# An mLSTM cell and a multiplicative FFN on one core: the denominators' product on GpSimd, and three more units of y by way of DRAM

## The chip, the core and the metric

The kernel runs on one core of one Trainium2 chip, all in float32. The core has five engines, each with a queue of its own that it works through in order: TensorE (PE; loading weights, PEld, overlaps its matmuls), VectorE (DVE), ScalarE (ACT), GpSimd (POOL) and SyncE (SP), which here only issues DMAs. They meet at semaphores. The metric is the device time in microseconds, the median of several executions. Durations and starts below come from one profiled execution; starts are counted from the start of its span.

## The reference

For each of 4 batches and 8 heads an mLSTM cell runs over 768 steps; its output, laid out as 3072 tokens x 320, goes through a feed-forward net that multiplies two linear maps.

```python
for t in range(S):
    m_new = np.maximum(f_gate[:, :, t] + m, i_gate[:, :, t])
    f_stab = np.exp(f_gate[:, :, t] + m - m_new)
    i_stab = np.exp(i_gate[:, :, t] - m_new)
    C = f_stab * C + i_stab * outer(v_t, k_t)
    n = f_stab * n + i_stab * k_t
    h_tilde, nq = C @ q_t, n . q_t
    denom = np.maximum(np.abs(nq), 1.0)
    y[:, :, t] = sigmoid(o_gate[:, :, t]) * h_tilde / denom
x = y.transpose(0, 2, 1, 3).reshape(3072, 320)
out = ((x @ w1) * (x @ w2)) @ w3 @ w_out          # d_ff = 1024
```

(The loop is shortened: indices of batch and head are left out.)

## The kernel before

**Units and passes.** The steps are cut into chunks of 64, and two chunks of one batch make a *unit*: 128 tokens, all 8 heads. There are 24 units; unit n is batch n % 4, pair of chunks n // 4. One loop, `for s in range(len(n_up))`, makes 32 *passes*. Pass s loads ahead for units s + 2 and s + 3, does the scores and the state update of unit s, the outputs of unit s - 1, brings the output of an earlier unit into the layout that the FFN needs, and puts FFN work in between. Four units, one for each batch, make a *group* of 512 tokens; the FFN works group by group.

**The cell in a pass (`quarter_work`).** PE multiplies into two PSUM tiles `cell`: for unit n = s - 1 the weighted values (`ph`) and what the states before give (`pi`); for unit s the scores (`ss`) and the two states' increments (`pc`). All matmuls are recorded on L92, all transposes by PE on L95. DVE then goes through this list, in this order:

- L423, L430 (four): `h` = `pi` times a gate column, plus `ph`. `h` has 41 columns a head; the 41st is the denominator's sum.
- L438: absolute value of that column, into `den`.
- L397: scores of unit s times their weights (`first_read`: what follows is issued after it).
- L440: maximum with 1, times 2.
- L404 (L406 for the first four units): first increment into `state`; POOL then multiplies this state by its decay (L335, `decayed`), into the next state.
- L441: reciprocal of `den`.
- L414: second increment into that next state. It waits for L335.
- L443: `e = (tanh + 1) * den`, in place in `o_in`, with `den` broadcast over a head's 40 columns.
- L445: `y = h * e`.

`outputs` is a generator that hands out the `den` steps one at a time, so that `quarter_work` can put other work between them; `late` is a hook that in pass 3 converts a piece of the weights (`convert`: L199, L200) at two places of the list, the second time the remainder `wr`. The last four units have one increment only, so no L335 and L414 in the middle.

**From y to x.** The FFN needs y with the features on the partitions. There are two ways. Units below `NY` = 15: POOL copies the last 64 columns a second time (`twice`, L476), PE transposes three blocks of 128 columns (`x_trans`, L95, tile `px`), ACT copies the result to `xT` (L486). Units from `NY` on: SP writes y to DRAM in four DMAs (`send`, L456 and L458), reads it back in four, with 32x32 blocks in place (`get_back`, L465, one buffer `yb`), and DVE turns the blocks (`x_turn`, L472). In pass s that is for unit s - 2, `send` at the pass's head, `get_back` after the pass's loads, `x_turn` after the outputs. Units 12 to 15 are the fourth group, of which three now go through PE.

**SP's queue.** In a pass SP issues `send`, the rows of U for `pw` of unit s + 3 (L159), k, v and o for unit s + 2 (L139, L153), `get_back`, then k and q of unit s + 2 in turned blocks (`load_turned`, L148), which DVE transposes in the next pass (`turn`, L317). Each waits for its data or buffer and holds up what is behind it.

**POOL's queue.** In a pass: L335 for the decay of the state, a second L335 in the middle of the cell's work, `vw` (L330, values times weights, for the next unit), masks on `pw` (L308, two), and `twice`. In passes 16 and 17 come four sums of weights each (L659).

**The FFN.** Groups 0 to 2 are computed straight (`up`, L638, L639). Groups 3 to 5 go by seven products instead of eight (`up_by_seven`): DVE makes four differences of tokens a group (`token_sums`, L666, into `w3T`), in passes 17, 21 and 25; PE makes the products; ACT copies two of them to `wo` (L702, L704, called `kept`), DVE adds (L686, L684), POOL finishes `kept` (L711, two), DVE adds the rest (L686, L684, into `a_sb` and `ab`), and POOL multiplies the two halves (L729, two). The same is done for the output (`out_by_seven`), with sums of the output weights on POOL (L755, one in pass 24, three in pass 25) and of `ab` on DVE (`ab_sums`, L770). The code puts L729 and L755 behind the outputs of the pass:

```python
        with tc.issue_after(gated.ins) if gated else nullcontext():
            if seven:
                seven[3]()
            for _ in range({NU: 1, NU + 1: 3}.get(s, 0)):
                next(wsums)
```

**What sets the order.** PE's order is the order of the code (`in_order`). Elsewhere each engine takes its instructions in the order in which they stand in its queue, which follows the code and the `issue_after` hints.

Of the kernel before, what the change touches and what calls it, by code (L numbers as in the profile page):

```python
# [11 lines left out]
OP = mybir.AluOpType  # L12
# [4 lines left out]
def kernel(  # L17
# [26 lines left out]
    nc = tc.nc  # L44

    B, H, S, D = q.shape
    L = 64
    P = 128
# [6 lines left out]
    DM = H * D  # L55
# [21 lines left out]
    def mps(shape, name):  # L77
        pool = banks.pop(0)
        banks.append(pool)
        return pool.tile(shape, FP, name=name, tag="m")  # L80
# [10 lines left out]
    def mm(out, lhsT, rhs, start=True, stop=True):  # L91
        in_order(nc.tensor.matmul(out, lhsT=lhsT, rhs=rhs, start=start, stop=stop))  # L92
# [4 lines left out]
    def warm(n, m=4, small=0):  # L97
        bank = mps([P, 4, P], "fill")
        for _ in range(n):
            mm(bank[:, 0:m], ident, ident.unsqueeze(1).to_broadcast([P, m, P]))  # L100
        for i in range(small):
            r = halves[i % 2]
            mm(bank[r, 0, 0:L], ident[r, 0:L], ident[r, 0:L])
# [8 lines left out]
    N_DIAG = 2  # L112
# [10 lines left out]
    decay = const.tile([P, B * NP, NT], FP, name="decay")  # L123
    UT = const.tile([P, 2, 3, BH], FP, name="UT")
    U_d = dram.tile([NT, BH, L], FP, name="U_d")
    NY = 15
    KC = KF + 1
    y_d = [dram.tile([P, 4, KC, 32], FP, name=f"y_d{n}") if n >= NY else None for n in range(NU)]

# [137 lines left out]
    qT_t, kT_t, vw_t, before_t, y_t, x_t = {}, {}, {}, {}, {}, {}  # L267
# [65 lines left out]
    def decayed(new, old, n, x):  # L333
        c, b = divmod(n, B)
        nc.gpsimd.tensor_tensor(out=new, in0=old, op=OP.mult, in1=decay[:, b * NP:(b + 1) * NP, 2 * c + x:2 * c + x + 1]  # L335
                                .to_broadcast([P, NP, D1]))

    def quarter_work(s, rest, between, late):


        rest()

        def part(j, c0, n):
            return cell[j][:, :, c0:c0 + NP * n].rearrange("p x (n d) -> p x n d", d=n)

        ss, pc, pi = part(0, 0, L), part(0, NP * L, D1), part(1, 0, D1)
        ph = [cell[1][:, x, NP * D1:2 * NP * D1].rearrange("p (h d) -> p h d", d=D1) for x in range(2)]
        n = s - 1
        if 0 <= n < NU:
            pw, vt, qT = u_t.pop(n), vbuf[n % NBV], qT_t.pop(n)  # L350
            before = before_t.pop(n)
            if n < N_DIAG:
                warm(1)

            if n < N_DIAG:
                ph = mps([P, H, D1], "ph")
                for hq in range(H):
                    for r in halves:
                        mm(ph[r, hq, :], pw[r, hq, :], vt[r, hq, :])
            for hd in range(H // 2 if n >= N_DIAG else 0):  # L360
                for x, e in quarters:
                    hq = hd if x == e else hd + H // 2
                    mm(ph[x][halves[e], hd, :], pw[halves[x], hq, :], vt[halves[x], hq, :])
            for p in range(NP):
                for hip, x in quarters if n >= B else quarters[1:3]:
                    mm(pi[halves[x], hip, p, :], qT[heads[hip], p, halves[x]], before[x][heads[hip], p, :])
        den = None
        if 0 <= s - 1 < NU:
            den = outputs(s - 1, pi, ph)
            den()  # L370
            if between:
                for _ in range(3):
                    den()
                den = None
                between()
            if late:
                late()
        n, first_read = s, None
        if n < NU:
            c, b = divmod(n, B)  # L380
            kt, vw = kbuf[n % NB], vw_t.pop(n)
            ends = range(2 if c < NT2 - 1 else 1)
            first, second, after = state[b]
            before_t[n] = first, second
            state[b] = after, second, first
            kT, qT, pw = kT_t.pop(n), qT_t[n], u_t[n]
            for p in range(NP):
                for hip, x in quarters:
                    mm(ss[halves[x], hip, p, :], kT[heads[hip], p, halves[x]], qT[heads[hip], p, halves[x]])
            M = D if n else L  # L390
            for p in range(NP):
                for x, e in quarters:
                    if x in ends:
                        mm(pc[e * L:e * L + M, x, p, :], kt[halves[x], 2 * p + e, 0:M], vw[halves[x], 2 * p + e, :])
        if n < NU:
            pv = pw.rearrange("p (n two) t -> p two n t", two=2)
            first_read = nc.vector.tensor_tensor(out=pv, in0=ss, in1=pv, op=OP.mult)  # L397
        with tc.issue_after(first_read.ins) if first_read else nullcontext():
            if den:
                den()  # L400
            if n < NU:

                if c:
                    nc.vector.tensor_tensor(out=second, in0=pc[:, 0], in1=second, op=OP.add)  # L404
                else:
                    nc.vector.tensor_copy(out=second, in_=pc[:, 0])  # L406
                if len(ends) > 1:
                    decayed(after, second, n, 1)
            if late:
                late()  # L410
            if den:
                den()
            if n < NU and len(ends) > 1:
                nc.vector.tensor_tensor(out=after, in0=pc[:, 1], in1=after, op=OP.add)  # L414
            if den:
                done = den()
        return done if den else first_read

    def outputs(n, pi, ph):
        c, b = divmod(n, B)  # L420
        hs = slice(b * H, (b + 1) * H)
        h = sb.tile([P, H, D1], FP, name="h", tag="h")
        nc.vector.tensor_tensor(out=h.rearrange("p (n two) d -> p two n d", two=2), in0=pi,  # L423
                                in1=gT[:, c, hs].rearrange("p (n two) -> p two n", two=2).unsqueeze(3)
                                .to_broadcast([P, 2, NP, D1]), op=OP.mult)
        if n < N_DIAG:
            nc.vector.tensor_tensor(out=h, in0=ph, in1=h, op=OP.add)
        for x, e in quarters if n >= N_DIAG else ():
            part = h[halves[x], 0:H // 2] if x == e else h[halves[x], H // 2:H]
            nc.vector.tensor_tensor(out=part, in0=ph[x][halves[e]], in1=part, op=OP.add)  # L430

        den = sb.tile([P, H, 1], FP, name="den", tag="den")

        def steps():
            V = nc.vector
            yield V.tensor_scalar(out=den.bitcast(U32), in0=h[:, :, D:D1].bitcast(U32), scalar1=0x7FFFFFFF, scalar2=None,  # L438
                            op0=OP.bitwise_and)
            yield V.tensor_scalar(out=den, in0=den, scalar1=1.0, scalar2=2.0, op0=OP.max, op1=OP.mult)  # L440
            yield V.reciprocal(out=den, in_=den)  # L441
            e = o_t.pop(n)
            nc.vector.scalar_tensor_tensor(out=e, in0=e, scalar=1.0, in1=den.to_broadcast([P, H, D]), op0=OP.add, op1=OP.mult)  # L443
            y_t[n] = sb.tile([P, DM + REM], FP, name="y", tag="y")
            yield nc.vector.tensor_tensor(out=y_t[n][:, 0:DM].rearrange("p (h d) -> p h d", d=D), in0=h[:, :, 0:D],  # L445
                                           in1=e, op=OP.mult)

        done = steps()
        return lambda: next(done)

# [24 lines left out]
    def twice(n):  # L475
        nc.gpsimd.tensor_copy(out=y_t[n][:, DM:DM + REM], in_=y_t[n][:, KF * P:DM])  # L476
# [83 lines left out]
    V = nc.vector  # L560
# [7 lines left out]
    for i, r in enumerate(third):  # L568
        V.tensor_tensor_scan(out=M[r, 1:GC + 1], data0=F3[r, :, L - 1], data1=U3[r, :, L - 1], initial=M[r, 0:1],
                             op0=OP.add, op1=OP.max)  # L570
# [24 lines left out]
    for i, r in enumerate(third):  # L595
        nc.gpsimd.tensor_tensor(out=pick[r, :, i, :], in0=pair[r].to_broadcast([BH, B * NP, GC]), op=OP.mult,
                        in1=dec[r].unsqueeze(1).to_broadcast([BH, B * NP, GC]))
# [222 lines left out]
    for s in range(len(n_up)):  # L820
        if NY <= s - 2 < NU:
            send(s - 2)
# [19 lines left out]
        if s < NU:  # L842
            if s >= B:
                decayed(state[s % B][1], state[s % B][0], s, 0)
        if s == 2 or N_DVE < s < NY + 2:
            twice(s - 2)
        if NY <= s - 2 < NU:
            get_back(s - 2)
        while s >= N_DVE and turned < min(s - 2, NY):
            x_trans(turned)  # L850
# [32 lines left out]
        def rest():  # L883
            for x in open_ups:
                up_rest(*x)
            if seven:
                seven[2]()
            if s == 3:
                scale_next()
                scale_next()  # L890
# [27 lines left out]
        with tc.issue_after(gated.ins) if gated else nullcontext():  # L918
# [4 lines left out]
            if s == NU + 1:  # L923
                ab_sums(*summed.pop(0))
            if NY <= s - 2 < NU:
                x_turn(s - 2)
# [85 lines left out]
```

## Time and profile before

| | |
|---|---|
| time, median of 3 runs | 426.37 us (426.09 to 426.73) |
| profiled execution, span | 425.8 us |
| mean granted clock of TensorE | 0.996 |
| DMA moved | 51.15 MB, mean 120 GB/s |
| L443, DVE, 24 times | 17.4 us, 725 ns each (491 to 1295) |
| L445, DVE, 24 times | 17.0 us, 709 ns each (491 to 1443) |
| L330, POOL, 24 times | 18.3 us, 764 ns each (730 to 1177) |
| L335, POOL, 40 times | 20.0 us, 500 ns each (462 to 775) |
| L472, DVE, 9 times | 5.1 us, 570 ns each |
| transposes for `px`, PE, 45 matmuls | 8.5 us, 295 ns each (they overlap) |
| L486, ACT, 15 times | 7.0 us, 468 ns each |
| L476, POOL, 15 times | 3.7 us, 244 ns each |

A line of a time line has the start in us, the length in us, the engine, the line of the kernel, the operation, output and inputs, the shapes and how many instructions are merged; in brackets stands how long the engine was idle before, and who ended that. Instructions of one engine overlap a little, so a start may come before the end of the one ahead. Matmuls are pipelined and their ends are modelled: their starts are the safer numbers. "issue" as a releaser means that the profile shows nothing that was waited for.

### The profile page before, as it was taken

Reading aid. Unit: us, or ns where it says so; the run is one execution under the profiler, and the core shown is the slowest. Engines: PE = TensorE matmul, PEld = TensorE weight load, DVE = VectorE, ACT = ScalarE, POOL = GpSimd, SP = SyncE. Lnnn points to the kernel's source line nnn. Section 1 sums busy time; section 2 is a strip of 40 time slices with the busy share of each in tenths; the row PEclk is TensorE's granted clock in tenths of the full one; section 3 lists DMA queues with packets and bytes.
Section 4 is the critical chain, followed back from the end, with each engine's and each line's share of the span. In section 5 each row is a group of like instructions: output and inputs, shape, how many; then the busy total and the mean of one; then the engine's idle time right before and its main releaser. Section 6 shows DMA issues by size and latency. Waiting matters only on the chain.

```text
span 425.8 us, 13079 instructions
## 1 busy us (share of the span) xinstructions
PE 414.1 (97%) x5353; PEld 335.3 (79%) x5353; DVE 313.5 (74%) x635; ACT 150.1 (35%) x404; POOL 154.3 (36%) x211
## 2 busy tenths in 40 slices
PE   7989989999999999999999999999999999999996
PEld 4768878888688788787777778788778879888896
DVE  6676986888949779778736966596868699575971
ACT  4766865567723623630433313032311110210000
POOL 4421342233303303303307751546453587542100
PEclk9989999999999999999999999999999999999999
DMA  8999998598977776985425675756421120000001
GB/s 186 204 173 245 214 144 140 134 193 180 215 183 154 166 182 135 181 164 105 89 80 130 153 141 121 142 133 117 87 44 36 35 39 2 31 2 31 2 32 62
DMA packets 135211, 51.15 MB, mean 120 GB/s; under 512 B 109360, under 2 KB 126960, under 8 KB 135152
## 3 DMA queue, kind: packets, MB, share of 16 engines
q1 hardware_dynamic: 131552, 46.29, 53.9%
q10 hardware_dynamic: 3600, 4.03, 2.7%
q8 instruction: 42, 0.69, 0.7%
q14 instruction: 17, 0.14, 0.1%
HBM read 44.50 MB, written 5.80 MB: 118 GB/s over the span
## 4 chain that ended last, share of the span: by engine, by line
PE 53%; issue 20%; DVE 7%; POOL 7%; SPq 7%; DMA 5%; ACT 1%; POOLq 0%; DVEq 0%
PE cell L92 17%; PE pa L92 12%; PE o L92 8%; PE pb L92 8%; PE p L92 3%; POOL pw L308 3%; SPq L184 3%; DVE w3T L666 2%; PE pt L95 1%; POOL vw L330 1%; SPq L148 1%; DMA raw<-in_moe_w_dram 1%; PE fill L92 1%; POOL raw L659 1%; POOL state L335 1%
## 5 line engine op out<-in xcount | busy, mean ns | idle before, releaser
L335 POOL TENSOR_TENSOR state<-state,decay 128x164 f32<-128x164 f32 x40 | 20.0, 500 | 154.8 <-DVE state L404 129.0
L92 PE MATMUL pa<-xT,w 128*128 128x256 f32 x240 | 60.4, 382 | 0.0
L92 PEld LDWEIGHTS pa<-xT,w 128*128 128x128 f32 x240 | 44.4, 190 | 6.8 <-DVE h L430 0.4
L303 ACT ACTIVATE pw<-pw,aT 128x64 f32<-128x64 f32 x184 | 46.4, 339 | 3.2 <-ACT o_sb L741 1.9
L92 PE MATMUL pb<-xT,w 128*128 128x256 f32 x192 | 45.4, 379 | 0.0
L729 POOL TENSOR_TENSOR ab<-ab,a_sb 128x512 f32<-128x512 f32 x22 | 29.4, 1356 | 32.2 <-DVE ab L684 32.2
L92 PEld LDWEIGHTS pb<-xT,w 128*128 128x128 f32 x192 | 36.4, 190 | 5.0
L711 POOL TENSOR_TENSOR wo<-wo 128x512 f32<-128x512 f32 x22 | 27.4, 1268 | 29.8 <-DVE wo L686 29.8
L92 PE MATMUL pa<-xT,wr 64*64 64x256 f32 x384 | 37.0, 386 | 0.5 <-DVE wr L200 0.5
L92 PE MATMUL wp<-wo,w3T 128*128 128x320 f32 x128 | 35.9, 433 | 1.1 <-DVE ab L639 0.6
L308 POOL TENSOR_SCALAR_AFFINE_SELECT pw<-pw 64x512 f32<-64x512 f32 x48 | 35.8, 746 | 3.0 <-ACT pw L303 1.2
L92 PE MATMUL pb<-xT,wr 64*64 64x256 f32 x384 | 36.4, 380 | 0.0
L92 PE MATMUL cell<-w3o,ab 128*128 128x320 f32 x128 | 35.4, 432 | 0.0
L638 ACT ACTIVATE a_sb<-pa 128x512 f32<-128x512 f32 x24 | 14.3, 598 | 59.0 <-PE pb L92 59.0
L639 DVE TENSOR_TENSOR ab<-pb,a_sb 128x512 f32<-128x512 f32 x24 | 16.4, 688 | 23.2 <-ACT a_sb L638 22.8
L92 PEld LDWEIGHTS wp<-wo,w3T 128*128 128x128 f32 x128 | 23.8, 190 | 10.5 <-DVE ab L639 0.8
L92 PEld LDWEIGHTS cell<-w3o,ab 128*128 128x128 f32 x128 | 24.3, 190 | 9.5
L92 PEld LDWEIGHTS pa<-xT,wr 64*64 64x64 f32 x384 | 18.9, 132 | 15.4 <-issue 8.8
L686 DVE SCALAR_TENSOR_TENSOR a_sb<-pa,wo 128x512 f32<-128x512 f32 x12 | 8.3, 689 | 29.8 <-PE pa L92 29.8
L430 DVE TENSOR_TENSOR h<-cell,h 64x164 f32<-64x164 f32 x88 | 28.6, 326 | 1.6
L92 PE MATMUL po<-w3o,ab 128*128 128x320 f32 x96 | 26.4, 433 | 0.0
L92 PEld LDWEIGHTS po<-w3o,ab 128*128 128x128 f32 x96 | 18.1, 190 | 7.3
(180 smaller groups left out, 846.4 us busy)
## 6 DMA issues: line engine op xcount, KB each, us to landing
raw<-in_moe_w_dram SPq DMA_DIRECT2D x64, 128.0 KB, 3.4
kbuf<-in_k_dram SPq DMA_DIRECT2D x24, 160.0 KB, 4.5
v_all<-in_v_dram SPq DMA_DIRECT2D x24, 160.0 KB, 4.9
o_in<-in_o_gate_dram SPq DMA_DIRECT2D x24, 160.0 KB, 4.8
pw<-U_d SPq DMA_DIRECT2D x28, 128.0 KB, 3.5
raw<-in_moe_w_dram SPq DMA_DIRECT2D x5, 512.0 KB, 6.7
raw<-in_moe_w_out_dram SPq DMA_DIRECT2D x8, 320.0 KB, 4.1
gates<-in_k_dram SPq DMA_DIRECT2D x28, 80.0 KB, 2.5
```

What stands on the lines that cost most here:

```text
L92: in_order(nc.tensor.matmul(out, lhsT=lhsT, rhs=rhs, start=start, stop=stop))
L184: nc.sync.dma_start(out=dst, in_=src)
L303: nc.scalar.activation(out=pw[:, h, :], in_=src[:, h, :], func=AF.Exp, bias=aT[:, c, b * H + h:b * H + h + 1])
L308: nc.gpsimd.affine_select(out=pw[r], in_=pw[r], compare_op=OP.is_ge, fill=0.0, base=0, pattern=[[0, H], [1, L]], channel_multiplier=-1)
L335: nc.gpsimd.tensor_tensor(out=new, in0=old, op=OP.mult, in1=decay[:, b * NP:(b + 1) * NP, 2 * c + x:2 * c + x + 1] .to_broadcast([P, NP, D1]))
L430: nc.vector.tensor_tensor(out=part, in0=ph[x][halves[e]], in1=part, op=OP.add)
L638: nc.scalar.mul(out=a_sb, in_=pa, mul=UP ** -2)
L639: nc.vector.tensor_tensor(out=ab_t[gr][j][:, fs[0]:fs[-1] + 1, t0:t0 + a_sb.shape[-1]], in0=pb, in1=a_sb, op=OP.mult)
L666: nc.vector.tensor_tensor(out=dst, in0=p, in1=q, op=OP.subtract)
L686: nc.vector.scalar_tensor_tensor(out=out, in0=p, scalar=UP ** -2, in1=q, op0=OP.mult, op1=OP.add)
L711: aside_by.tensor_tensor(out=kept[j][:, 1:4:2], in0=kept[j][:, 1:3], in1=kept[j][:, 3:4].to_broadcast([128, 2, TH]), op=OP.add)
L729: aside_by.tensor_tensor(out=t[:, f:FO:FH, :], in0=t[:, f:FO:FH, :], in1=a, op=OP.mult)
```

## The change

Two things are changed.

First, from unit 2 on (`N_DIAG` = 2) the order of the products is another: `h * den` is made in place by POOL, and DVE then makes y from `tanh`, 1 and that product in one instruction. The reciprocal and POOL's product are issued right after the maximum, before the first increment of the state; y itself stays at the end of the list. Units 0 and 1 keep the two products on DVE.

Second, `NY` is 12 instead of 15: units 12, 13 and 14 go through DRAM and DVE as the later ones do.

```diff
--- before.py
+++ after.py
@@ -123,7 +123,7 @@
     decay = const.tile([P, B * NP, NT], FP, name="decay")
     UT = const.tile([P, 2, 3, BH], FP, name="UT")
     U_d = dram.tile([NT, BH, L], FP, name="U_d")
-    NY = 15
+    NY = 12
     KC = KF + 1
     y_d = [dram.tile([P, 4, KC, 32], FP, name=f"y_d{n}") if n >= NY else None for n in range(NU)]
 
@@ -398,6 +398,8 @@
         with tc.issue_after(first_read.ins) if first_read else nullcontext():
             if den:
                 den()
+                if s - 1 >= N_DIAG:
+                    den()
             if n < NU:
 
                 if c:
@@ -408,7 +410,7 @@
                     decayed(after, second, n, 1)
             if late:
                 late()
-            if den:
+            if den and s - 1 < N_DIAG:
                 den()
             if n < NU and len(ends) > 1:
                 nc.vector.tensor_tensor(out=after, in0=pc[:, 1], in1=after, op=OP.add)
@@ -438,12 +440,18 @@
             yield V.tensor_scalar(out=den.bitcast(U32), in0=h[:, :, D:D1].bitcast(U32), scalar1=0x7FFFFFFF, scalar2=None,
                             op0=OP.bitwise_and)
             yield V.tensor_scalar(out=den, in0=den, scalar1=1.0, scalar2=2.0, op0=OP.max, op1=OP.mult)
-            yield V.reciprocal(out=den, in_=den)
+            done = V.reciprocal(out=den, in_=den)
             e = o_t.pop(n)
-            nc.vector.scalar_tensor_tensor(out=e, in0=e, scalar=1.0, in1=den.to_broadcast([P, H, D]), op0=OP.add, op1=OP.mult)
             y_t[n] = sb.tile([P, DM + REM], FP, name="y", tag="y")
-            yield nc.vector.tensor_tensor(out=y_t[n][:, 0:DM].rearrange("p (h d) -> p h d", d=D), in0=h[:, :, 0:D],
-                                           in1=e, op=OP.mult)
+            y, hn, all_d = y_t[n][:, 0:DM].rearrange("p (h d) -> p h d", d=D), h[:, :, 0:D], den.to_broadcast([P, H, D])
+            if n < N_DIAG:
+                yield done
+                V.scalar_tensor_tensor(out=e, in0=e, scalar=1.0, in1=all_d, op0=OP.add, op1=OP.mult)
+                yield V.tensor_tensor(out=y, in0=hn, in1=e, op=OP.mult)
+            else:
+                nc.gpsimd.tensor_tensor(out=hn, in0=hn, in1=all_d, op=OP.mult)
+                yield done
+                yield V.scalar_tensor_tensor(out=y, in0=e, scalar=1.0, in1=hn, op0=OP.add, op1=OP.mult)
 
         done = steps()
         return lambda: next(done)
```

In the changed kernel's code the lines behind the first edit are numbered 2 to 8 higher.

## The prediction

> **What bounds the kernel now.** I read first the page's busy times, then the waits of PE, then the time line of each engine around every place where PE waited.
>
> ```profile
> PE 414.1 (97%) x5353; PEld 335.3 (79%) x5353; DVE 313.5 (74%) x635; ACT 150.1 (35%) x404; POOL 154.3 (36%) x211
> ```
>
> PE is busy for 414.1 of 425.8 us, at a granted clock of 0.996, so time is won only by taking work from PE or by ending one of its few waits. The waits of PE that lie in the changed region (engine and line that waited, who released it, us in total, times, longest):
>
> ```profile
> PE cell L92 <- issue: 1.9, 2, 1.5
> PE pa L92 <- DVE wr L200: 0.5, 1, 0.5
> PE pa L92 <- DVE w3T L666: 0.4, 1, 0.4
> PE o L92 <- DVE wo L686: 0.2, 1, 0.2
> ```
>
> Three of them end with VectorE (DVE), at 47.33, 242.83 and 356.12 us; there a DVE that is later makes PE later. Everywhere else from 60 us on PE runs on without a gap, and DVE or POOL may be late by their slack without cost.
>
> **Part 1: the transposes that leave PE.** The time line of PE, with a unit's x_trans (220.07) and one pass later without:
>
> ```profile
> 219.65 0.49 PE L92 MATMUL cell<-vw,kbuf 64*40 64x41 f32 x32
> 220.07 0.55 PE L95 MATMUL px<-ident,y 128*128 128x128 f32 x3
> 220.46 8.78 PE L92 MATMUL po<-w3o,ab 128*128 128x320 f32 x32
> ...
> 230.61 0.49 PE L92 MATMUL cell<-vw,kbuf 64*40 64x41 f32 x32
> 231.03 1.34 PE L92 MATMUL po<-w3o,ab 128*128 128x320 f32 x4
> ```
>
> From the start of the cell matmuls to that of po it takes 0.81 us with the three transposes and 0.42 without: 0.39 us a unit. Units 12, 13 and 14 lose them: 3 x 0.39 = **-1.17 us**. ACT also loses three copies (L486, 0.47 each) and POOL three small ones (L476, 0.24), on engines with idle time there. What takes their place: per unit 8 DMA issues on SP (4 at L456 and L458, some 2.4 us; 4 at L465, 1.7 to 6.4 us) and one DVE transpose (L472, 0.57). SP has room: it waits 10.2 us, from 214.6 to 224.9, for unit 15's y. The new wait is send(13), for y of unit 13 at about 194.6, while SP stood at 188.5 before; behind it queue unit 18's pw, unit 17's k, v and o, the read-back and unit 17's turned k and q. The last go out at about 203 instead of 195.65, and DVE turns them at 224.79: covered by 20 us. send(14) puts unit 18's turned loads at about 218 instead of 210.93, needed at 236.37. Were that cover gone, the lateness would go to PE one to one. The DVE transposes lie in passes where DVE idles 2.1 us or more. I cost these at nothing.
>
> **Part 2: the product that moves to POOL.** In 22 units one DVE instruction goes (L443; 0.49 us where POOL is quiet, 0.76 beside vw, up to 1.29), the other stays in length (L445 becomes a three-operand one), and POOL gets a product of 128x320. No row shows it; it is bounded by L335 (128x164, 0.46) below and vw at L330 (128x328, also with a broadcast, 0.73 alone, 1.18 beside DVE) above. I take **0.72**, the size of vw. The Trainium skill ("GPSIMD Engine Reference", section "Engine selection") speaks against it: it puts element-wise products on VectorE and GpSimd at about twice its time. By that it would be 0.98 (twice 0.49) and the sum 0.26 later; the row says 1.5 times.
>
> The saving on DVE is lost again in an ordinary pass, because the order in which the changed kernel's instructions stand on POOL has the product ahead of the state's decay, which DVE awaits:
>
> ```profile
> 233.31 0.20 DVE L441 RECIPROCAL den<-den 128x8 f32<-128x8 f32 x1
> 233.47 0.46 POOL L335 TENSOR_TENSOR state<-state,decay 128x164 f32<-128x164 f32 x1 [2.50 <-DVE state L404]
> 233.97 0.33 DVE L414 TENSOR_TENSOR state<-cell,state 128x164 f32<-128x164 f32 x1 [0.47 <-POOL state L335]
> 234.22 0.76 DVE L443 SCALAR_TENSOR_TENSOR o_in<-o_in,den 128x320 f32<-128x320 f32 x1
> 235.01 0.82 DVE L445 TENSOR_TENSOR y<-h,o_in 128x320 f32<-128x320 f32 x1
> ```
>
> With the reciprocal done at 233.39, the product runs 233.45 to 234.18, the decay to 234.62, L414 starts at 234.64 instead of 233.97, y ends at about 235.65 instead of 235.83. In the early passes, where L445 takes 0.49, y ends 0.2 later instead. Both are hidden where DVE then waits for PE or ACT (0.9 to 7.6 us). POOL's vw, masks and decay move back by 0.7; they are used a pass (8 to 18 us) later. Three places have no cover:
>
> *Pass 3 (47.33).* The reciprocal and the product now come before convert() of wr, for which PE waits. DVE's L199 moves from 45.99 to 46.24 (+0.25), into the product (46.13 to 46.85). A row for such a meeting: at 65.28 L199 took 0.58 instead of 0.32 beside L335. The custom L200 took 0.90 beside POOL at 88.30, 0.49 at its best. So +0.25 +0.2 +0.2 = **+0.65**; bounds 0 (the unexplained 1.5 us wait of PE at 57.57 absorbs it) and +0.85. The Trainium skill ("SBUF — State Buffer", section "Who interferes with whom") lets the instruction that starts first keep the shared port until it ends and blocks the other fully; by that L199 would start at 46.85 and the term be about 0.85. The rows show partial progress.
>
> *Pass 17 (242.83).* The first four token sums (L666) end 0.2 sooner by the chain above, but the four weight sums on POOL (L659, 236.43 to 241.85) end 0.7 later, and L666 takes 1.1 to 1.5 beside them against 0.43 alone. Only the last L666 (0.68) was nearly free of them. I take **+0.3**; bounds -0.41 (the wait goes) and +0.6.
>
> *The tail (356.12).* Here unit 23's product enters a chain that POOL limits:
>
> ```profile
> 335.68 2.50 POOL L729 TENSOR_TENSOR ab<-ab,a_sb 128x512 f32<-128x512 f32 x2 [4.06 <-DVE ab L684]
> 338.14 1.54 POOL L755 TENSOR_TENSOR v_all<-w3o 128x640 f32<-128x640 f32 x1
> 338.24 1.47 DVE L440 TENSOR_SCALAR den<-den 128x8 f32<-128x8 f32 x1
> 342.40 2.50 POOL L711 TENSOR_TENSOR wo<-wo 128x512 f32<-128x512 f32 x2 [2.71 <-DVE wo L686]
> 343.71 0.69 DVE L686 SCALAR_TENSOR_TENSOR a_sb<-pb,wo 128x512 f32<-128x512 f32 x1
> 344.93 0.69 DVE L684 TENSOR_TENSOR ab<-pb,wo 128x512 f32<-128x512 f32 x1
> 356.12 1.35 PE L92 MATMUL o<-w3o,ab 128*128 128x160 f32 x8 [0.22 <-DVE wo L686]
> ```
>
> POOL keeps its order, so L729, ready at 335.68, stands behind the product. The maximum at 338.24 is no longer held up by L755 (0.16 instead of 1.47), so the reciprocal ends at 338.63 and the product runs 338.70 to 339.42. Then L729 (2.74 beside the new y, as at 264.61) to 342.1, L755 (1.54) to 343.6, L711 (2.50) to 346.1. The second L684 needs both halves of L711: 346.15 instead of 344.93, **+1.22**. From there DVE works without a gap (four L770, a transpose, four L666) to the L686 that PE awaits at 356.12, so PE is later by as much. Bounds: +0.95 (L729 at its 2.50) and +1.7 (the product at vw's 1.18). In passes 20 to 22 L729 stands behind the product too, some 3.7 us later, but L711 then ends about 1.1 us before its reader, since DVE waits for PE there.
>
> **The sum.** -1.17 + 0.65 + 0.3 + 1.22 = +1.0. The profiled execution's span is 425.8, giving 426.8; the median of 426.37 lies 0.57 above that span, so **427.3 us**. The low ends give -1.17 + 0 - 0.41 + 0.95 = -0.63 (425.7), the high ends -1.17 + 0.85 + 0.6 + 1.7 = +1.98 (428.4).
>
> **The rivals.** 0.2% is 0.85 us, about what a measurement of this kernel can tell from no change; 427.22 is that bound.
> *Forecast, slower (0.50):* PE gains 1.17 and pays more at the three DVE waits, the tail first. 427.3, own range 427.2 to 428.4.
> *Even (0.35):* the tail's +1.22 just cancels the transposes, and pass 3 is absorbed at 57.57 or the product is shorter: -1.17 + 1.22 + 0.3 = +0.35, 426.7. For it: the terms are close in size. Against it: wr's conversion ends straight before PE's start.
> *Faster (0.15):* DVE, not POOL, limits the tail. If freeing L440 (1.3) and L443 (0.49) brings L686 forward at 356.12, that wait goes too, and the one at 242.83 as well: -1.17 - 0.41 - 0.22 = -1.8, 424.6. It decides from the point where POOL ends L711 by 344.9. For it: L440's 1.47 does vanish. Against it: POOL's work from 338.70 on adds up to 7.4 us without a pause.
> *The order on POOL is not kept* (inside the even case): the product has its place after the decay, so pass 17 loses nothing and the tail +0.2. The listing of the changed kernel speaks against it.
>
> The range, 425.5 to 428.4, takes in both ends of the sum and leaves out most of the faster case and little above.
>
> **What would show it.** Three px groups fewer, and cell to po in 0.42 at 204.8 and 220. L335 starting about 0.7 after the reciprocal's end, and L414 behind it. PE's wait for L200 at 47 grown from 0.5 to about 1.1; for L666 near 242 to 0.7; for L686 near 356 to 1.4. In the tail L711 starting about 1.2 later against PE. The forecast is wrong if L711 there starts as early as before, or if PE waits at a new place, such as for a turned k or q near 236 or for xT of the fourth group.

## The result and the profile after

The changed kernel took 435.74 us (median of 4 runs, 435.00 to 437.64) against 426.27 us (4 runs) for the kernel before: a ratio of 1.0236, 95% interval 1.0214 to 1.0259. It is slower by some 9.5 us, where the prediction had +0.9 and a range that ended at 428.4. The profiled execution of the changed kernel has a span of 433.6 us, 7.8 more than before.

From the page of the changed kernel: PE's busy time, and the clock granted to it in 40 slices of the span.

```profile
PE 413.7 (95%) x5344; PEld 335.5 (77%) x5344; DVE 301.6 (70%) x616; ACT 148.5 (34%) x401; POOL 168.6 (39%) x230
...
PEclk9999999999999999999999799999999999999999
```

PE is busy as long as before (414.1) although it lost 9 transposes, so some of its work ran slower; and its idle time has grown by 8.2 us. DVE lost 11.9 us of work, POOL gained 14.3. One slice, around 245 us, has a clock of about 0.7. The waits of the changed kernel that matter (who waited, for whom: us in total, times, longest):

```profile
DVE xT L480 <- DMA yb<-y_d: 22.2, 6, 7.0
PE cell L92 <- DVE qT L317: 4.1, 2, 3.7
...
PE o L92 <- DVE wo L694: 1.4, 1, 1.4
PE pa L92 <- DVE wr L200: 1.3, 1, 1.3
```

The first line was 1.4 us, once, before; the second is new. They point at a place that the prediction did not price: the transpose of the read-back `yb` (L480, L472 before).

**Where the time went.** L397, one DVE instruction, stands once in each pass up to 23, so its start after less its start before, pass by pass, is the drift of the whole kernel. This table is worked out from the time lines of all the kernels in this document (e1 to e10 are the experiments below):

```
start of L397 less that of before, us, in pass
                                9      14      17      18      20      23   17 to 20
after                       +0.41   +0.39   -0.34   +3.40   +6.50   +6.48   +6.84
e1  product alone           +4.03   +4.48   +4.47   +5.02   +6.23   +6.22   +1.76
e2  three units alone       -3.43   -2.95   -3.73   +2.85   +4.57   +4.65   +8.30
e3  after, stores on POOL   -0.29   -0.15   -0.99   -0.44   +0.77   +0.79   +1.76
e4  read-back at once       -1.18   -0.77   -1.61   +0.50   +2.70   +6.05   +4.31
e5  e2, stores on POOL      -2.95   -2.68   -3.52   -3.36   -3.36   -3.33   +0.16
e6  before, stores on POOL  -2.33   -1.57   -1.57   -1.45   -1.44   -1.46   +0.13
e7  e3, decay first         +1.43   +1.77   +0.93   +1.82   +3.60   +3.62   +2.67
e8  e3, units 2, 23 on DVE  -1.25   -1.23   -2.08   -1.52   -0.30   -0.28   +1.78
e9  turn first              -3.10   -3.08   -3.92   +0.33   +3.83   +3.91   +7.75
e10 e5, five units          -2.76   +6.72   +5.87   +6.02   +6.02   +6.02   +0.15
```

In the changed kernel 6.84 of the 7.8 us are lost between passes 17 and 20. The column for pass 9 shows something else: up to there the kernels are largely alike, yet single executions lie 7 us apart (e1's had a granted clock of 0.54 from 20 to 30 us). Beside the experiments the kernel before took 424.5 to 429.5 us (medians 425.9 to 426.5). So medians tell one or two us at best here, and mechanisms are read from the drift between two passes.

**The place itself.** SP's queue of the changed kernel, with what it did for units 14 and 15:

```profile
203.84 2.90 SPq L148 DMA_DIRECT2D q_all<-in_k_dram  x4
206.83 2.19 SPq L148 DMA_DIRECT2D q_all<-in_q_dram  x4
209.85 1.24 SPq L464 DMA_DIRECT2D y_d<-y  x2
211.14 6.28 SPq L466 DMA_DIRECT2D y_d<-y  x2
...
229.60 2.69 SPq L464 DMA_DIRECT2D y_d<-y  x2
...
237.42 3.35 SPq L473 DMA_DIRECT2D yb<-y_d  x4
```

Two issues on L466 take 1.14 us elsewhere in this stretch; here 6.28. The waits of SP's queue name the cause, and ACT's time line shows it:

```profile
SPq L466 <- DMA out_dram<-o_sb: 8.6, 3, 5.2
```

```profile
213.84 0.43 ACT L749 COPY o_sb<-po 128x320 f32<-128x320 f32 x1 [3.87 <-PE po L92]
214.29 0.38 ACTq L751 DMA_DIRECT2D out_dram<-o_sb  x1
```

SP's last transfer of unit 14 goes at 217.03. The store of an output block that ACT issues at 214.29 has landed at 217.01, and both transfers report to the same completion semaphore (the one that a transfer raises when it has landed); the stores of this stretch take 2.4 to 3.3 us to land. In the trace, between 200 and 232 us, the transfers of SP and ACT take eight completion semaphores in turn, and a transfer waits until the one that held its semaphore before, about the eighth ahead of it in this rotation, has landed. So SP may not run far ahead of ACT's stores, and these wait for PE. SP came late to unit 15's `send` (229.60 instead of 224.90), so the read-back came late. In the kernel before, this chain closed without slack:

```profile
224.90 1.28 SPq L456 DMA_DIRECT2D y_d<-y  x2
226.22 1.15 SPq L458 DMA_DIRECT2D y_d<-y  x2
...
231.05 3.05 SPq L465 DMA_DIRECT2D yb<-y_d  x4
```

```profile
235.87 0.58 DVE L472 STREAM_TRANSPOSE xT<-yb 128x384 f32<-128x384 f32 x1
```

In the changed kernel DVE and PE stood:

```profile
242.34 0.58 DVE L480 STREAM_TRANSPOSE xT<-yb 128x384 f32<-128x384 f32 x1 [7.01 <-DMA yb<-y_d]
242.84 1.05 DVE L317 STREAM_TRANSPOSE kT<-gates 128x512 f32<-128x512 f32 x1
243.74 1.05 DVE L317 STREAM_TRANSPOSE qT<-gates 128x512 f32<-128x512 f32 x1
```

```profile
244.84 1.13 PE L92 MATMUL cell<-qT,kT 40*64 40x64 f32 x32 [3.69 <-DVE qT L317]
245.75 0.77 PE L92 MATMUL cell<-vw,kbuf 64*40 64x41 f32 x32
246.45 1.22 PE L92 MATMUL pa<-xT,w 128*128 128x256 f32 x2
```

The last line took 0.70 in the kernel before. The stretches of the changed kernel (start:end, then busy times; the third number from the right is the granted clock) tell why:

```profile
242.00:244.00 2.00, 0.00 (x0) 0.00 (x0) 1.66 (x3) 1.40 (x6) 0.15 (x1) 0.86 0.42 115
244.00:246.00 2.00, 1.16 (x48) 1.16 (x52) 1.97 (x5) 0.00 (x0) 0.00 (x0) 0.50 0.48 139
246.00:248.00 2.00, 2.00 (x36) 1.65 (x29) 1.89 (x7) 0.00 (x0) 0.00 (x0) 0.50 0.61 141
248.00:250.00 2.00, 2.00 (x6) 1.58 (x5) 1.27 (x5) 0.00 (x0) 0.81 (x2) 0.50 0.43 66
```

While PE stood, its clock fell to 0.50, and it stayed there until 250.25, for 5.4 us of PE's work. From the first product behind the wait (244.84) to the last one before the clock came back (250.02) PE needed 5.2 us; the same products took 3.0 us before (240.80 to 244.23, without the wait of 0.41 in between). That is some 2.2 us on top of the wait.

My theory before the experiments: the first part of the change makes this loss, through SP's wait for ACT's stores. The rivals: A, the product on POOL makes y late, and with it SP; B, SP's queue is simply full (21 issues a pass, some 14.6 us); C, memory traffic delays the read-back.

### The profile page after: what moved, and what is told of

It reads as the page before. It is cut to its first block, busy times and chain, and to the rows that moved or that the text cites. A ratio compares the mean times of both kernels' runs of the same rounds, so it can differ in the third digit from the quotient of the medians.

```text
span 433.6 us, 13095 instructions
## 1 busy us (share of the span) xinstructions
PE 413.7 (95%) x5344; PEld 335.5 (77%) x5344; DVE 301.6 (70%) x616; ACT 148.5 (34%) x401; POOL 168.6 (39%) x230
## 3 DMA queue, kind: packets, MB, share of 16 engines
q10 hardware_dynamic: 3600, 4.03, 2.7%
## 4 chain that ended last, share of the span: by engine, by line
PE 76%; DVE 7%; SPq 7%; DMA 4%; issue 3%; ACT 1%; POOL 1%; DVEq 0%; POOLq 0%; ACTq 0%
PE cell L92 20%; PE pa L92 19%; PE pb L92 13%; PE wp L92 8%; PE o L92 8%; PE p L92 3%; SPq L139 3%; PE po L92 3%; SPq L184 2%; DMA raw<-in_moe_w_dram 1%; DMA wo<-in_moe_w_dram 1%; DVE pw L778 1%; PE px L95 1%; PE pt L95 1%; DVE h L432 1%
## 5 line engine op out<-in xcount | busy, mean ns | idle before, releaser
L452 POOL TENSOR_TENSOR h<-h,den 128x320 f32<-128x320 f32 x22 | 15.9, 724 | 170.2 <-DVE den L443 170.2
L92 PE MATMUL pa<-xT,w 128*128 128x256 f32 x240 | 61.4, 387 | 0.0
L737 POOL TENSOR_TENSOR ab<-ab,a_sb 128x512 f32<-128x512 f32 x22 | 30.6, 1415 | 13.2 <-DVE ab L692 13.2
L308 POOL TENSOR_SCALAR_AFFINE_SELECT pw<-pw 64x512 f32<-64x512 f32 x48 | 34.3, 714 | 1.6
L646 ACT ACTIVATE a_sb<-pa 128x512 f32<-128x512 f32 x24 | 14.3, 597 | 59.8 <-PE pb L92 59.8
L454 DVE SCALAR_TENSOR_TENSOR y<-o_in,h 128x320 f32<-128x320 f32 x22 | 21.2, 963 | 3.4 <-POOL h L452 3.4
```

What stands on the lines that cost most here:

```text
L308: nc.gpsimd.affine_select(out=pw[r], in_=pw[r], compare_op=OP.is_ge, fill=0.0, base=0, pattern=[[0, H], [1, L]], channel_multiplier=-1)
L452: nc.gpsimd.tensor_tensor(out=hn, in0=hn, in1=all_d, op=OP.mult)
L454: yield V.scalar_tensor_tensor(out=y, in0=e, scalar=1.0, in1=hn, op0=OP.add, op1=OP.mult)
L646: nc.scalar.mul(out=a_sb, in_=pa, mul=UP ** -2)
L737: aside_by.tensor_tensor(out=t[:, f:FO:FH, :], in0=t[:, f:FO:FH, :], in1=a, op=OP.mult)
```

## The experiments

**e1: the product alone.** The changed kernel with the first part undone.

```diff
-    NY = 12
+    NY = 15
```

> The changed kernel with its first part undone (NY = 15 again, the product by the reciprocal on GpSimd kept). My theory (the loss of 6.8 us at passes 17 to 19 comes from part 1: SP's queue, lengthened by the DMAs of units 12 to 14, brings yb late): no wait of DVE for yb beyond the 1.4 us of before, no wait of PE for a turned qT over 0.5 us, and of the loss only pass 3 (+0.9), pass 17 (0 to +0.3) and the tail (+1.25) stay: 428.3 to 428.9 us. Rival A (the product makes y late, and a late y makes SP late): the waits for yb and qT stay, 434 to 436 us.

Measured: 432.65 us (6 runs, 429.19 to 435.33), ratio 1.013, interval 1.0083 to 1.0177. The median fits neither number. In the profiled execution (435.33 us) the front of the kernel is late, +4.03 at pass 9; the two executions with a mean granted clock of 1.000 took 429.19 and 429.87 us, close to what was expected of the product alone. Whether the front explains the other three is not shown. The trace decides: PE has no listed wait for a turned qT, and the drift from pass 17 to 20 is +1.76, not +6.84. Rival A falls for the large loss. But 1.76 is more than the 0.3 that I expected of the product here; PE's time line of e1 shows what of:

```profile
247.85 0.70 PE L92 MATMUL pa<-w3T,w 128*128 128x256 f32 x2 [0.96 <-DVE w3T L674]
...
252.38 1.99 PE L92 MATMUL cell<-w3T,raw 128*128 128x256 f32 x8 [0.37 <-DVE state L416]
...
271.42 1.99 PE L92 MATMUL cell<-w3T,raw 128*128 128x256 f32 x8 [0.33 <-DVE state L416]
```

The token sums cost 0.55 more than before (0.96 against 0.41). The two waits for L416 are new: the matmul ahead of each started 0.97 and 0.92 earlier instead of 0.43, so they cost 0.54 and 0.49.

**e2: the three units alone.** The kernel before with `NY = 12`.

> The kernel before with the first part alone (NY = 12, the product by the reciprocal stays on VectorE). My theory: the waits for yb near 228, 242 and 256 us, PE's wait for qT near 244 (3 to 4 us) and the fallen clock behind it are all there; -0.8 from the transposes and +6.8: 431 to 433 us. Rival A (the product is needed for it): no wait for qT, -0.8 to -1.2: 425.1 to 425.6 us.

Measured: 433.79 us (6 runs), ratio 1.0178, interval 1.0138 to 1.0219, a little above the 431 to 433 that I expected. PE waits 6.5 us for qT and the clock falls; from pass 17 to 20 it loses 8.30. The first part alone makes the loss. It is even larger than in the changed kernel, so the costs of the two parts do not simply add (8.30 and 1.76 alone, 6.84 together): SP issues unit 15's read-back by 237.62, 3.15 us sooner than there, yet DVE gets `yb` only 0.55 sooner, at 241.79. Why that read-back took so much longer to land I have not settled; traffic may have a share in it.

**e3: the stores by another queue.** The changed kernel; the stores of the first ten output blocks go out by GpSimd, which takes completion semaphores of its own.

```diff
-            nc.scalar.dma_start(out=out[t0:t0 + P, :], in_=o_sb)
+            (nc.gpsimd if (gr, j) < (2, 2) else nc.scalar).dma_start(out=out[t0:t0 + P, :], in_=o_sb)
```

> The changed kernel with the stores of the first ten output blocks issued by GpSimd's queue in place of ScalarE's; bytes and order of the loads are unchanged. My theory (send(14)'s last transfer stands 5.2 us on SP at 212 us because it may not go before a store of ScalarE's, eighth before it among the transfers that share completion semaphores, has landed): the 5.2 us at 212 and the 6.7 us at 258 go, send(15) goes out at about 225 in place of 229.6, DVE waits for yb under 1.5 us, PE's wait for qT goes and the clock stays at 1.0: 428.5 to 430 us, less up to 1 us for GpSimd's issues. Rival B (SP is full: 21 issues a pass, some 14.6 us, are as long as a pass, whatever the stores do): send(15) stays at 229 or later, 434 to 436 us. Rival C (the memory traffic at 225 to 240 us delays yb): no change either.

Measured: 429.58 us (10 runs), ratio 1.0072, interval 1.0043 to 1.0102. SP's queue in e3, and DVE's transpose of unit 15:

```profile
209.31 1.24 SPq L464 DMA_DIRECT2D y_d<-y  x2
210.59 1.14 SPq L466 DMA_DIRECT2D y_d<-y  x2
...
224.58 1.25 SPq L464 DMA_DIRECT2D y_d<-y  x2
```

```profile
236.10 0.58 DVE L480 STREAM_TRANSPOSE xT<-yb 128x384 f32<-128x384 f32 x1 [1.42 <-DMA yb<-y_d]
```

The 6.28 has become 1.14, unit 15 goes out at 224.58, PE's wait for qT is gone and no slice's clock falls. From pass 17 to 20 it loses 1.76, exactly what the product costs in e1: the first part's 5.1 us (6.84 - 1.76) are gone, with the same transfers and bytes. Rivals B and C fall for these 5.1 us; that SP has almost no idle time left between 209 and 249 in e3 speaks for B as the next limit. The Trainium skill ("DMA: Bandwidth & Descriptors", section "Issuing engines are not separate DMA queues") says that issuing transfers from several engines saves only the issuing time on the sequencer. The stores' issues take 0.34 to 0.39 us each on ACT, which was not late; the 5.1 us come out of SP's wait for these stores, so here the measurement goes beyond that statement.

**e4: the read-back at once.** SP's order alone: `get_back` straight behind `send`.

```diff
         if NY <= s - 2 < NU:
             send(s - 2)
+            get_back(s - 2)
```

> The changed kernel with the read-back of a unit issued straight behind its send, ahead of the pw, k, v and o loads (SP's order alone). My theory: the block at 212 and so send(15) at 229.6 stay, but yb of unit 15 lands 2 to 3.5 us sooner than at 242.3; PE's wait for qT falls from 3.7 to 0.3 to 1.7 us: 430 to 433 us. If SP's fullness alone decided (rival B), the read-back gains what the loads lose and the turned loads are late next: within 1 us of 435.7.

Measured: 436.51 us (4 runs), ratio 1.0252, interval 1.0202 to 1.0302. PE's wait for qT falls, but to 2.57 and not to the 0.3 to 1.7 that I expected, and 2.5 us are won between passes 17 and 20; but 3.4 are lost again between 20 and 23. SP's waits for the stores did not go, they moved to the turned loads (6 times, 13.3 us in all) and others. The expected time was missed, and the time lies where rival B had it (within 1 us of 435.7). This run therefore does not tell my theory from rival B; e3 does. What it shows is that this reordering of SP does not pay while the stores still stand in front.

**e5 and e6: the first part with free stores, and the control.** e5 is the kernel before with `NY = 12` and e3's edit, e6 the kernel before with e3's edit alone.

> The kernel before with the first part of the change (NY = 12) and the stores of the first ten output blocks on GpSimd's queue; the product stays on VectorE. My theory (the first part costs only through SP's wait for ScalarE's stores): no wait of PE for qT, at most 2 us of waits of DVE for yb near 236 and 249, from pass 9 to pass 20 a change against before of -0.7 (the transposes): 0.6 to 0.9 us below the kernel before. Rival B (SP is full with the 24 more transfers): at least 1 us of PE's wait for qT stays, slower than before.

> Control: the kernel before with the stores of the first ten output blocks on GpSimd's queue and nothing else (NY = 15). My theory: SP's waits for these stores (11.0 us in all in the kernel before) go, but they stood in front of nothing that was late, so the time stays: within 0.4 us of before. If moving the stores were a gain or a loss by itself, this shows its size.

Measured: e5 424.92 us (12 runs), ratio 0.9979, interval 0.9961 to 0.9996; e6 426.11 us (12 runs), ratio 0.9993, interval 0.9965 to 1.0021. e6 is no different from before: the kernel before had waits for stores on SP as well (11.0 us in four on L465, 4.0 in two on L139), but nothing late stood behind them. (In e6, 6.1 us in two are left on L465, for later stores that still go by ACT.) e5 loses next to nothing from pass 17 to 20 (+0.16), wins 0.84 from 14 to 17, and is the only version measured as faster than the kernel before, by about 0.2% (its interval just leaves out 1). Its median is 1.6 us below, more than the 0.6 to 0.9 expected and the 0.7 that these passes show; the rest lies within what the front spreads.

**e7: the decay ahead of the product.** e3, with the product issued behind L335.

```diff
-                nc.gpsimd.tensor_tensor(out=hn, in0=hn, in1=all_d, op=OP.mult)
                 yield done
+                yield nc.gpsimd.tensor_tensor(out=hn, in0=hn, in1=all_d, op=OP.mult)
...
-            if den and s - 1 < N_DIAG:
+            if den:
                 den()
```

> The kernel of e3_outputs_by_gpsimd with the product issued behind the state's decay on GpSimd. My theory of part 2 (between pass 17 and 20 it costs 1.76 us, because the decay stands behind the product: 0.55 more of the wait for the token sums, and two waits of PE for the state's addition, about 0.5 us each, since that addition frees a PSUM bank that the seven-product matmuls write): the waits for state near 247 and 266 go, the wait for w3T falls from 0.97 to 0.4 or less, and pass 3 loses its 0.9 too, since the product comes behind wr's conversion there: drift from pass 17 to 20 under +0.5 in place of +1.76, in all 1.5 to 2.5 us below e3_outputs_by_gpsimd; the tail's +1.25 stays. Rival D (the weight sums on GpSimd and their port set the token sums): the wait for w3T stays near 1.0.

Measured: 430.97 us (6 runs), ratio 1.0097, interval 1.006 to 1.0135. Half right. PE's wait for wr in pass 3 fell from 1.3 to 0.7, both waits for L416 are gone, and the drift from pass 19 to 20 is +0.09 instead of +0.57. But the wait for the token sums did not fall, it grew, and the clock fell with it:

```profile
244.65 1.05 PE L92 MATMUL pa<-w3T,w 128*128 128x256 f32 x2 [1.31 <-DVE w3T L674]
245.50 1.06 PE L92 MATMUL pb<-xT,raw 128*128 128x256 f32 x2
```

My account of the token sums was wrong. They stand behind unit 15's transpose of `yb`, for which DVE waits 0.66 us in e1, 1.42 in e3 and 1.69 in e7, and run beside POOL's weight sums; the decay's place does not set them. What DVE saves on the product it spends waiting for `yb`.

**e8: the first and the last unit back on DVE.** e3, with the two old products for units 2 and 23.

```diff
-            if n < N_DIAG:
+            if n < N_DIAG or n in (2, NU - 1):
                 yield done
```

(The two conditions in `quarter_work` are changed alike.)

> The kernel of e3_outputs_by_gpsimd with the product of unit 2 and of unit 23, the first and the last that had moved, back on VectorE. My theory: PE's wait for the adds (L694) near 357 falls from 1.4 to 0.2 and the tail's +1.25 goes; PE's wait for wr near 47 falls from 1.3 to 0.5, worth 0.5 to 0.9; passes 17 to 20 keep their +1.76: 1.7 to 2.2 us below e3_outputs_by_gpsimd. If the tail's loss came from units 20 to 22, where the product also stands before L737, it stays.

Measured: 427.31 us (12 runs), ratio 1.0024, interval 0.9994 to 1.0053: 2.27 below e3, where I expected 1.7 to 2.2. The tail's wait and wr's conversion in e8:

```profile
355.99 1.35 PE L92 MATMUL o<-w3o,ab 128*128 128x160 f32 x8 [0.33 <-DVE wo L694]
```

```profile
45.66 0.43 DVE L199 TENSOR_SCALAR wr<-raw 128x512 uint32<-128x512 uint32 x1
46.23 0.73 DVE L200 CUSTOM_DVE_ANT_0 wr<-raw,wr 128x1024 uint16<-128x1024 uint16 x1
```

The tail's wait is 0.33 instead of 1.43, so it was unit 23's product alone. From the start of L397 to the end of L200 on wr it is 2.26 us here (44.70 to 46.96), 2.94 in the changed kernel, where L199 took 0.97, and 2.19 before.

**e9: VectorE's order.** The changed kernel with the turn of k and q ahead of the transpose of `yb`.

```diff
-            if NY <= s - 2 < NU:
-                x_turn(s - 2)
...
                 gated = turn(s + 1)
+            if NY <= s - 2 < NU:
+                x_turn(s - 2)
```

> The changed kernel with VectorE's turn of k and q of the next unit issued ahead of the transpose of yb (VectorE's order alone; the stores stay on ScalarE's queue). In the changed kernel the turned k and q near 242 wait behind a transpose that waits 7.0 us for yb, though their own data landed by 232. My theory: PE's wait for qT near 244 goes, yb still lands at about 242, and PE waits for the token sums (w3T) in its place, some 2.5 us later in its pass: 1.5 to 3 us of wait for w3T, the clock still falls to 0.5 for a few us; drift from pass 17 to 20 of +3 to +5 in place of +6.84, 432 to 434 us. Rival (the late k and q themselves, not VectorE's order, hold PE): the wait for qT stays at 3 us or more.

Measured: 434.46 us (4 runs), ratio 1.0188, interval 1.0147 to 1.0229. The wait for qT is gone, and another of 4.66 us has taken its place a little later:

```profile
243.16 1.22 PE L92 MATMUL pa<-w3T,w 128*128 128x256 f32 x2 [4.66 <-DVE w3T L674]
```

The drift from pass 17 to 20 is +7.75; I had expected +3 to +5. So the order on DVE is not to blame: the token sums need the same `yb` in the same pass, and reordering only changes the name under which PE waits.

**e10: five units.** e5 with `NY = 10`.

> The kernel of e5 (product on VectorE, stores of the first ten blocks on GpSimd) with NY = 10: units 10 and 11 too leave PE, so five units of 8 more transfers each on SP. My theory (the transposes are worth 0.27 us of PE each, and SP keeps up as long as no store stands in front): passes 12 to 20 of PE run as in e5 and 0.4 to 0.6 us less: 424.3 to 424.7 us. Rival B (SP is full): yb or turned loads come late from pass 12 on, a new wait of PE of 1 us or more, 426 us or more.

Measured: 436.08 us (6 runs), ratio 1.0249, interval 1.0202 to 1.0295. Both expectations missed the reason. Passes 14 to 20 run as in e5 (-0.70), with no wait for a turned load; but units 10 and 11 belong to the third group, whose second half PE multiplies at the head of pass 14:

```profile
182.93 3.75 PE L92 MATMUL pa<-xT,w 128*128 128x256 f32 x8 [7.08 <-DVE xT L472]
```

That is 9.3 us between passes 13 and 14. Units 12 to 14 can go by DRAM only because PE takes up their group in pass 19, not before.

## Why the prediction was wrong

- **"I cost these at nothing"** (the DMAs that take the transposes' place). This is the step that failed, and most of the error: 5.1 of the 6.8 us by which the span grew more than the +1.0 of the sum (e3 against the changed kernel; e2 shows the loss without the product). I read the 10.2 us for which SP waits for unit 15's y as room. It was the start of a chain with no slack: in the kernel before y goes out at 224.90, the read-back's issues end at 234.10, and DVE turns `yb` at 235.87 straight behind y. I gave a deadline to the turned loads behind the new sends (met: unit 18's went out by 229.51) and none to the read-back itself.
- **SP's issues at their usual length.** I moved them past each other as if they waited only for their data. The wait for ACT's stores stood in the waits of SP's queue before (11.0 us in four on L465, 4.0 in two on L139); I didn't ask what decides where it falls.
- **"Were that cover gone, the lateness would go to PE one to one."** Too little: PE lost 3.7 us of wait and some 2.2 by the clock that fell behind it.
- **The transposes, -1.17.** Measured -0.73 in the changed kernel, -0.84 in e3 and e5 (passes 14 to 17). The gap from cell to po does shrink by 0.39, but po behind it takes 8.88 instead of 8.78 us, and from its start to the next pass's cell it is 8.82 instead of 8.70 (231.03 to 239.85, 220.46 to 229.16, both before the change). I read only the starts, and my fence broke the second row off after four of its 32 products, so it could not show this.
- **Pass 3, +0.65.** On DVE +0.75 (2.94 against 2.19); e8 gives it back. The mechanism was right and the sum nearly, but not its parts: L199 lost 0.55 beside the product instead of 0.2 (last section), and L200, for which I had 0.2, took 0.73 as before. How much of it reaches the end is lost in the front's spread.
- **Pass 17, +0.3.** The wait for the token sums grew by 0.55, inside my bounds, but not for my reason (e7). I priced L335's and L414's delay and noted that DVE then waits for PE anyway; I did not see that L414 is also what frees the PSUM bank for which PE's seven-product matmuls wait. That is another 1.0 us (e1; e7 takes it away).
- **The tail, +1.22.** Right: the wait grew from 0.22 to 1.43, and e8 takes it away by one unit's product.
- **The product's length, 0.72.** Right: 0.724 on average over 22.

The sum with these sizes: -0.7 (transposes) + 0.75 + 1.76 (passes 17 to 20, product) + 1.2 + 5.1 (first part) = 8.1; the span grew by 7.8. The first part is taken here as what freeing the stores wins (e3); alone it cost 8.30 (e2). The medians lie 9.5 us apart, 1.7 more than the spans, and there my conversion failed: I put the median 0.57 above the profiled span, but in the executions of before whose span is on record the time lies about 2.0 us above the span of the same execution (1.7 to 1.8 in the changed kernel). The profiled execution of before was thus some 1.4 us slower than its median. The prediction's own warning, PE waiting near 236 for a turned k or q, came true at 241 (and for 0.41 us already at 230), but I had given it no price.

## What to carry to other kernels

When a queue is seen waiting, ask what the waited-for item starts: a wait at the head of a chain that ends just in time is no room. Before adding transfers to a queue, give the last transfer of each added chain (here the read-back) a deadline, and look in the waits of the issuing queue for transfers of other engines. And when an instruction is delayed on one engine, list all that it releases, PSUM banks too, not only its data's next reader.

## What was not expected of the hardware

- **A short wait of PE can cost its clock.** The granted clock fell to 0.50 around waits of PE of 1.31 (e7), 2.57 (e4), 3.69 (after), 4.66 (e9), 6.53 (e2) and 7.08 us (e10), and stayed there for 3.6 to 6.0 us after PE resumed; in e4 and e7 it fell only after PE was at work again. Each whole stretch at 0.50 lasted 3.4 us (e4, e7) or two or three times that (6.8 in after, e2 and e9, 10.2 in e10). Behind the waits of 0.96 to 0.98 us at the same place (e1, e3, e8) it stayed at 1.00, but so it did behind the changed kernel's waits of 1.30 us for wr (47.58) and 1.43 us in the tail (363.85). So the length of the wait alone does not decide; what else does, no run here shows. The Trainium skill ("TensorE: Matmul & The Clock Gate", section "Part 1: The HAM clock gate") has it fall after an idle window of about 3.4 us and come back after as long a busy one. The way back agrees roughly; the 1.31 us of e7 is much shorter than that window, and by the page's rule it would have cost nothing; there the measurement decides.
- **POOL holds DVE off more fully than I took it.** The two engines of the changed kernel in pass 3:

```profile
45.65 0.72 POOL L452 TENSOR_TENSOR h<-h,den 128x320 f32<-128x320 f32 x1 [8.04 <-DVE den L443]
```

```profile
45.68 0.97 DVE L199 TENSOR_SCALAR wr<-raw 128x512 uint32<-128x512 uint32 x1
```

L199 takes 0.43 us without the product (e8) and 0.97 beside it: of the 0.69 us of overlap it loses 0.54. The prediction preferred partial progress (0.2 lost) to the rule of a full block by the instruction that starts first, and that rule's 0.85 for the whole term was as near to the measured 0.75 as my 0.65.
